# A linear-attention and mixer kernel with another order: token weights before the fourth pair's rows, four banks for the mixers, a later end for the zero products, other seeds

## Chip, cores and metric

The kernel runs on one core of a Trainium2 chip. A core has five engines with a queue of instructions each: PE (TensorE: matmuls, with a separate row PEld for its weight loads), ACT (ScalarE), DVE (VectorE), POOL (GpSimd) and SP (SyncE, which here issues DMA transposes only). PE writes to PSUM, which has eight banks. The metric is the device time of one execution in microseconds (us); shown are medians of several executions.

## The reference, cut to what matters

Four batches of eight heads, 768 steps, 64 numbers a head. The first part is a linear attention with a decay for each head, the second a mixer over steps and then over channels:

```python
for t in range(S):                       # S = 768, per batch and head
    state = gamma * state + outer(k[t], v[t])
    y[t] = scale * q[t] @ state
x = y as [batch, 768, 512]               # the eight heads side by side
h = relu(x^T @ w_tok1) @ w_tok2          # w_tok1 768x256, w_tok2 256x768
u = x + h^T
out = u + relu(u @ w_ch1) @ w_ch2        # w_ch1 512x1536, w_ch2 1536x512
```

## The kernel before, in words

Steps are cut into 6 blocks of 128, heads into 4 pairs. Everything is float16 on its way into PE and float32 in PSUM. The work is written as operations (class Op), each with its engine (or a choice of engines), planned cost, what it depends on and the buffers and PSUM banks it takes.

The front of a batch and pair (function `front`) is: scale k by the decay (L443 on ACT or L445 on DVE); transpose k and q (L479, L477) and copy them out as kT and qT (L486); the block states k^T v (L501) and their running sum U (L510, L513), copied to r (L524); the products within a block (L550), masked to am (L564); Y from both (L580, L584), scaled to X (L598 on ACT, or L602 on DVE) and cast to x (L615). Then the token work: T1 = x with w_tok1 (L629, relu L639 or L641), T2 = with w_tok2 (L687, added to X at L694), cast to u (L702), transposed (L721) and copied out as uT (L727). For the third and fourth pair of the first batch ("turned") T2 is made already transposed (L654, L657) and copied to uT at L664. Pair p's T1 depends on the pair before having done its T2 where that has an L687; the second and third pair's do, the fourth's does not.

The back of a batch (function `back`) is the channel mixer: `widen` makes relu(u w_ch1) in 24 tiles (L777 on PE, L791 on ACT), `narrow` multiplies by w_ch2 (L819) and adds X (L828); for batches 2 and 3 `narrow_seven` does that with seven block products in place of eight (L896, L905). In the first batch a widen tile's products are planned as two halves, pairs 0 and 1 and pairs 2 and 3 (SPLIT).

All rows and weights are loaded by POOL's DMA queue, in the order in which `request` is called (L384 and L394 rows, L364 weights): k, q, v of each pair of the first batch, at most eight requests in flight. T1_AT and T2_AT say before which pair's rows the two token weights are requested; 4 is after the last. Then come the channel weights and the other batches' rows. For batches 2 and 3, SP transposes k, q and u by DMA.

PSUM banks come from sets by name (BANKS): the first batch's front takes banks 0 to 6, later fronts 0 to 4, the mixers 5 to 7; `narrow_seven` takes any of the eight. L550 of the later fronts takes four banks at once.

The order of all this is not written down but found when the program is built. `arrange` plans greedily: the operation that can start first, by priority. `replay` runs the planned order through a model with DMA landings and gives a planned time. This is repeated 16 times with landing times fed back, and then once for each seed in SEEDS: `shake` gives a random share of the operations a delay or a bias against an engine (what one seed sets stays for the next). The order with the least planned time is emitted. Each engine then executes its instructions strictly in that order.

At the very end (L1015 to L1025) products of zeros (L1023) are put into PE's order before an operation that the plan starts before F_ON ns with a planned gap over 400 ns before it: as many as fill 0.7 of the gap at 165 ns each. Their results are not used.

Of the kernel before, what the change touches and what calls it, by code (L numbers as in the profile page):

```python
# [18 lines left out]
def kernel(  # L19
# [31 lines left out]

    BUFS = dict(kf=6, qf=6, k16=3, v16=8, kT=4, qT=4, U=2, q16=3, r16=3, am=8, X=3, x16=5, h1=3, u16=3,
                uT=3, h2=2, o=4, w1=2)
    BANKS = dict(first=range(0, 7), front=range(0, 5), back=range(5, 8), seven=range(0, 8), fill=range(7, 8))
    SEM = 80
    XB, XU = 2, 2
    QH, TN = (1,), 2
    SEEDS = [20000, 20001, 20017, 20030, 20091, 20125]
    SPLIT, T1_AT, T2_AT = 1, 4, 4
    XS, M4 = 1, 3  # L60
    EARLY, BOTH_FIRST, SEVEN = 0, 1, 2
    ops = []
# [26 lines left out]
    def replay(order):  # L89
# [4 lines left out]
        for o in order:  # L94
# [3 lines left out]
            for s in o.takes:  # L98
                if s.tag in BANKS:
                    got.append(bank_of[s.bank])  # L100
# [82 lines left out]
    def arrange():  # L183
# [10 lines left out]
        def freed(slot):  # L194
            if slot is None:
                return 0
            if any(u.end is None for u in slot.users):
                return None
            return max(u.end for u in slot.users) + SEM

        while todo:
            best = []
            for op in todo:
# [7 lines left out]
                for s in op.takes:  # L211
                    if s.tag in BANKS:
                        got = [(t, i) for i in BANKS[s.tag] if i not in [x[1] for x in banks]
                               for t in [freed(bank_of[i])] if t is not None]
# [42 lines left out]
            for s in op.takes:  # L257
                if s.tag in BANKS:
                    s.bank = banks.pop(0)[1]
# [733 lines left out]
    def shake(seed):  # L993

        rng = random.Random(seed)
        share = rng.choice((0.005, 0.02, 0.06))
        for o in ops:
            if rng.random() < share:
                o.delay = rng.choice((0, 0, 200, 500, 1000, 2000))
                o.skew = {w[0]: rng.choice((0, 0, 300, 800)) for w in o.ways}  # L1000

    best = None
    for turn in range(16 + len(SEEDS)):
        if turn >= 16:
            shake(SEEDS[turn - 16])
        order = arrange()
# [4 lines left out]
    for o, o.start, o.end, o.eng, o.emit, at in best[1]:  # L1011
        for s, s.bank in zip(o.takes, at):
            pass
        order.append(o)
    FILL, F_ON, F_NS = 0.7, 30000, 165  # L1015
    spare, pe_at = None, 300
    for o in order:
        if o.eng == "PE":
# [37 lines left out]
```

## Time and profile before

| | us |
|---|---|
| median of 8 executions | 202.84 |
| lowest, highest | 202.35, 206.94 |
| the profiled execution | 202.35 |
| its span in the trace | 200.6 |
| PE, DVE, ACT, POOL busy | 192.0, 131.2, 111.6, 81.9 |

The page's rows of 40 slices, each some 5 us, show where the engines are busy (a digit is the busy share in tenths; 9 is 90% or more) and which share of TensorE's clock was granted:

```profile
PE   7979799999999999999999999999999999999991
PEld 3546587566777676656765566656767886567881
DVE  7359963018999998575797509476389984056972
ACT  3159786677898555538850583448766003775000
POOL 7997776388986953443381021212220100000100
PEclk9999999999999999999999999999999999999999
```

A busy PE in these rows includes the products of zeros: 63 matmuls of line L1023, the last of them at 29.6 us. In the waits listed for PE there are four entries:

```profile
PE bank L580 <- ACT r L524: 1.2, 4, 0.7
PE bank L1023 <- DVE zero L309: 1.1, 1, 1.1
PE bank L479 <- DVE k L445: 1.1, 1, 1.1
PE bank L777 <- ACT uT L727: 0.8, 1, 0.8
```

The columns are who waited for whom, us in total, how often, and the longest.

### The profile page before, as it was taken

The page shows a single profiled execution, that of the slowest core. Times are in us where ns is not written, and L with a number is a line of the kernel's source. Part 1 is how long each engine was busy: PE and PEld are TensorE (multiplying, and loading weights), DVE is VectorE, ACT ScalarE, POOL GpSimd, SP SyncE. Part 2 cuts the span into 40 slices and gives each one's busy share as a digit, 9 for nine tenths or more (in the row PEclk, how much of TensorE's full clock was granted, in tenths as well). Part 3 has the DMA queues.
Part 4 walks back from the last instruction along what each step waited for, and adds up shares of the span by engine and source line. Part 5 has one row for each costly group of instructions (what it writes and reads, how often), then busy time and mean ns, then how long its engine had stood idle before and what let it go on. Part 6 is the DMA issues. An engine that isn't in the chain of part 4 may idle for free.

```text
span 200.6 us, 5027 instructions
## 1 busy us (share of the span) xinstructions
PE 192.0 (96%) x2015; PEld 132.1 (66%) x2015; DVE 131.2 (65%) x344; ACT 111.6 (56%) x245; POOL 81.9 (41%) x114
## 2 busy tenths in 40 slices
PE   7979799999999999999999999999999999999991
PEld 3546587566777676656765566656767886567881
DVE  7359963018999998575797509476389984056972
ACT  3159786677898555538850583448766003775000
POOL 7997776388986953443381021212220100000100
PEclk9999999999999999999999999999999999999999
DMA  6999999999999999999999996360220052000143
GB/s 43 144 156 158 205 207 207 191 155 154 147 146 149 180 126 158 167 189 130 184 150 137 149 160 135 92 171 16 41 43 0 3 209 105 0 3 0 52 158 109
DMA packets 101607, 24.71 MB, mean 123 GB/s; under 512 B 94288, under 2 KB 98640, under 8 KB 101584
## 3 DMA queue, kind: packets, MB, share of 16 engines
q0 software_dynamic: 78784, 13.37, 100.6%
q1 hardware_dynamic: 19200, 4.72, 19.4%
q10 hardware_dynamic: 3600, 6.29, 10.4%
q8 instruction: 16, 0.26, 0.6%
q14 instruction: 7, 0.06, 0.1%
HBM read 26.74 MB, written 6.29 MB: 165 GB/s over the span
## 4 chain that ended last, share of the span: by engine, by line
PE 87%; ACT 6%; DVE 4%; issue 0%; DVEq 0%; ACTq 0%
PE bank L777 32%; PE bank L819 16%; PE bank L896 13%; PE bank L1023 5%; PE bank L629 5%; PE bank L687 5%; PE bank L550 3%; PE bank L584 2%; PE bank L580 2%; PE bank L501 2%; PE bank L479 2%; DVE am L564 1%; ACT X L598 1%; ACT r L524 1%; ACT uT L664 1%; ACT kT L486 1%
## 5 line engine op out<-in xcount | busy, mean ns | idle before, releaser
L777 PE MATMUL bank<-uT,wc 128*128 128x384 f16 x384 | 68.9, 326 | 0.8 <-ACT uT L727 0.8
L791 ACT ACTIVATE h<-bank 128x384 f16<-128x384 f32 x96 | 46.8, 491 | 30.0 <-PE bank L777 29.4
L777 PEld LDWEIGHTS <-wc 128*128 128x128 f16 x384 | 35.5, 98 | 22.3 <-issue 1.0
L564 DVE TENSOR_TENSOR am<-bank,mask 128x384 f16<-128x384 f32 x64 | 33.1, 550 | 5.4 <-PE bank L550 5.4
L819 PE MATMUL bank<-wc,h 128*128 128x512 f16 x144 | 36.4, 379 | 0.0
L615 POOL CAST x<-X 128x384 f16<-128x384 f32 x25 | 12.7, 509 | 35.8 <-ACT X L598 31.9
L598 ACT ACTIVATE X<-bank,gy 128x192 f32<-128x192 f32 x58 | 20.7, 421 | 5.0 <-PE bank L584 4.6
L694 DVE TENSOR_TENSOR X<-X,bank 128x384 f32<-128x384 f32 x28 | 14.3, 550 | 12.8 <-PE bank L687 12.6
L702 POOL CAST u<-X 128x384 f16<-128x384 f32 x22 | 11.0, 512 | 23.1 <-DVE X L694 23.1
L819 PEld LDWEIGHTS <-h 128*128 128x128 f16 x144 | 12.7, 98 | 10.3
L513 DVE SCALAR_TENSOR_TENSOR U<-U,gp,bank 128x64 f32<-128x64 f32 x64 | 17.7, 276 | 1.1
L524 ACT ACTIVATE r<-U 64x320 f16<-64x320 f32 x27 | 12.6, 467 | 10.1 <-DVE k L445 5.2
L384 POOL DMA_DIRECT2D kf<-in_k_dram x16 | 16.6, 1039 | 2.9 <-DMA qf<-in_q_dram 1.4
L905 POOL TENSOR_TENSOR o<-X,o 128x256 f32<-128x256 f32 x2 | 1.5, 726 | 39.5 <-DVE o L905 39.5
L384 POOL DMA_DIRECT2D v<-in_v_dram x16 | 16.5, 1032 | 1.8 <-DMA wc<-in_moe_w_ch_dram 1.4
L1023 PE MATMUL bank<-zero 128*128 128x384 f16 x63 | 14.6, 384 | 1.1 <-DVE zero L309 1.1
L896 PEld LDWEIGHTS <-h 128*128 128x128 f16 x144 | 14.1, 98 | 2.1
L584 PEld LDWEIGHTS <-am 128*128 128x128 f16 x192 | 12.3, 98 | 4.1 <-issue 1.6
L584 PE MATMUL bank<-v,am 128*128 128x64 f16 x192 | 14.2, 193 | 0.0
L629 PE MATMUL bank<-x,wt 128*128 128x128 f16 x192 | 13.2, 219 | 0.0
L580 PE MATMUL bank<-r,qT 128*128 128x128 f16 x80 | 11.9, 220 | 1.2 <-ACT r L524 1.2
L629 PEld LDWEIGHTS <-wt 128*128 128x128 f16 x192 | 11.7, 98 | 2.0 <-DVE uT L727 0.3
(89 smaller groups left out, 275.4 us busy)
## 6 DMA issues: line engine op xcount, KB each, us to landing
out_dram<-o ACTq DMA_DIRECT2D x23, 256.0 KB, 2.9
kf<-in_k_dram POOLq DMA_DIRECT2D x16, 192.0 KB, 8.6
v<-in_v_dram POOLq DMA_DIRECT2D x16, 192.0 KB, 8.5
wc<-in_moe_w_ch_dram POOLq DMA_DIRECT2D x6, 512.0 KB, 14.5
qf<-in_q_dram POOLq DMA_DIRECT2D x12, 192.0 KB, 8.9
wt<-in_moe_w_tok_dram POOLq DMA_DIRECT2D x2, 384.0 KB, 9.6
qf<-in_q_dram POOLq DMA_DIRECT2D x8, 96.0 KB, 8.3
out_dram<-o ACTq DMA_DIRECT2D x2, 128.0 KB, 1.9
```

Source lines behind the costliest of these rows:

```text
L384: nc.gpsimd.dma_start(out=tile_of(s, [P, 2, NC, D], F16), in_=src[b, 2 * p:2 * p + 2].rearrange("h (c p) d -> p (h c) d", p=P))
L513: nc.vector.scalar_tensor_tensor(U[:, c], U[:, c - 1], gp[:, p:p + 1], o, ALU.mult, ALU.add)
L564: nc.vector.tensor_tensor(am[:, :m], src, k_, ALU.mult)
L580: nc.tensor.matmul(o, QT.tile[:, c * P:(c + 1) * P], R[:, c - 1], start=True, stop=False)
L584: nc.tensor.matmul(o[:, j * D:(j + 1) * D], M.tile[:, m], V.tile[:, j, c], start=(c == 0), stop=(c == 0 or j == 1))
L598: nc.scalar.mul(X.tile[:, half(hf), h * D:(h + 1) * D], yv[:, :, j * D:(j + 1) * D], gy[:, h:h + 1])
L629: nc.tensor.matmul(acc[:, jt * P:(jt + 1) * P], wt1[:, i, jt * P:(jt + 1) * P], X16.tile[:, i], start=(i == 0), stop=(i == NC - 1))
L777: nc.tensor.matmul(acc[:, :SH], w[:, ct, (ft % FW) * P:(ft % FW + 1) * P], UT.tile[:, ct, sh * SH:(sh + 1) * SH], start=(ct == 0), stop=(c ...
L791: nc.scalar.activation(H2.tile[:, ft], A.tile[:, :SH], AF.Relu)
L819: nc.tensor.matmul(A.tile, H2.tile[:, ft, i * P:(i + 1) * P], wc2[ft // FW][:, ft % FW], start=(opens and ft == 0), stop=(ft == NF - 1), s ...
L896: nc.tensor.matmul(bank.tile[:, cols], lhs(f, t), rhs(f), start=(f == 0 and not adds), stop=(f == HF - 1), skip_group_check=adds)
L1023: nc.tensor.matmul(spare[:, :384], zero[:, :P], zero, start=True, stop=True)
```

## The change

It sets five constants. No operation is added or removed apart from products of zeros, whose number follows from the plan.

```diff
-    BANKS = dict(first=range(0, 7), front=range(0, 5), back=range(5, 8), seven=range(0, 8), fill=range(7, 8))
+    BANKS = dict(first=range(0, 7), front=range(0, 5), back=range(4, 8), seven=range(0, 8), fill=range(7, 8))
...
-    SEEDS = [20000, 20001, 20017, 20030, 20091, 20125]
-    SPLIT, T1_AT, T2_AT = 1, 4, 4
+    SEEDS = [10003, 10006, 10008, 10011, 10016, 10019, 10024, 10029, 10031, 10038, 10039, 10043,
...
+    SPLIT, T1_AT, T2_AT = 1, 3, 4
...
-    FILL, F_ON, F_NS = 0.7, 30000, 165
+    FILL, F_ON, F_NS = 0.7, 36000, 165
```

The list of seeds goes from 6 to 48 entries, none in common. The mixers' set of banks becomes 4 to 7; bank 4 stays in the later fronts' set too, so both draw on it. The first token weights are requested before the fourth pair's rows of the first batch and after the third's; the second token weights stay where they were, after the fourth's. Products of zeros are put into gaps that the plan has before 36 us instead of 30 us.

## Prediction

> **What bounds the kernel now.** I read the page first (busy shares, slices), then the busy time by stretches of the span, then the chain of waits in order of time, then the timeline of the first 36 us, then the landings of single loads. The stretches, cut at places that the chain gives (columns: stretch, its length, then busy time and instruction count of PE, PEld, DVE, ACT, POOL, then clock, DMA share, GB/s):
>
> ```profile
> 0.00:9.65 9.65, 8.52 (x37) 4.45 (x38) 5.39 (x35) 2.30 (x4) 8.52 (x13) 1.00 1.42 91
> 9.65:25.00 15.35, 12.86 (x223) 8.66 (x221) 12.45 (x38) 11.51 (x24) 12.66 (x17) 1.00 2.20 172
> 25.00:30.00 5.00, 4.82 (x80) 4.15 (x78) 3.10 (x9) 4.11 (x12) 3.50 (x7) 1.00 1.24 207
> 30.00:35.57 5.57, 4.80 (x68) 4.03 (x66) 1.76 (x4) 3.89 (x8) 3.92 (x6) 1.00 1.24 207
> 35.57:196.60 161.03, 160.96 (x1619) 110.77 (x1618) 108.03 (x259) 89.83 (x198) 53.26 (x74) 1.00 1.25 115
> 196.60:200.60 4.00, 0.00 (x0) 0.00 (x0) 0.47 (x2) 0.00 (x0) 0.00 (x0) 1.00 0.37 131
> ```
>
> From 35.57 us on PE is busy 160.96 of 161.03 us. It waits for nobody there, and its instructions are the same before and after the change, so that stretch can only get longer. The last 4.00 us are the last addition and its store. What can shrink is the time before 35.57. Of the 25.92 us from 9.65 to 35.57 PE is busy 22.48 and idle 3.44; 29 of its matmuls there are products of zeros, which follow each other at about 0.165 us when nothing else comes between: 4.8 us. So 8.2 us of PE are unused by the program: that is the ceiling of any gain. (The 34 zero products before 9.65 precede the first transpose, whose rows the change doesn't touch.) What fills those 8.2 us is the chain of waits (start, length, what):
>
> ```profile
> 28.03 0.22 PE bank L580
> 28.76 0.67 PE bank L629 x12
> 29.43 0.49 PE bank L1023 x3
> 29.92 0.34 PE bank L721 x6
> 30.26 0.71 PE bank L687 x12
> 30.97 1.34 PE bank L629 x24
> 32.31 0.35 PE bank L654 x2
> 32.86 0.48 ACT uT L664
> ...
> 34.82 0.71 ACT uT L727
> 35.57 9.10 PE bank L777 x55
> ```
>
> After the last pair's Y (L580/L584, done at 28.76) PE still owes the token work of pair 1 (L629, L687), pair 0's transpose (L721) and pair 2's L629, before pair 3's L629 and L654; then ACT copies uT five times in a row. The backlog exists because token work began late:
>
> ```profile
> 25.32 0.83 PE L629 MATMUL bank<-x,wt 128*128 128x128 f16 x12
> 25.99 1.14 PE L1023 MATMUL bank<-zero 128*128 128x384 f16 x6
> 26.96 0.83 PE L687 MATMUL bank<-h,wt 128*128 128x128 f16 x12
> ```
>
> Pair 0's L629 starts at 25.32, though its x was cast by 20.30 (the DVE cast L615 at 19.76 took 0.54): what it lacked was the first token weights. Landings, from two looks at single requests (the fourth pair's q and v, issued at 11.71 and 12.72, and the first token weights, issued at 13.72):
>
> ```profile
> DMA to landing us min/median/max: 7.9/8.2/8.5
> DMA to landing us min/median/max: 9.0/9.0/9.0
> ```
>
> So v of pair 3 landed at 21.2 and the weights at 22.7. By the same query k landed at 18.3, q at 19.6 and the second token weights at 24.6.
>
> **Part 1, the request moved (T1_AT 4 to 3).** The first token weights pass k, q and v of pair 3. Landings in POOL's queue follow one another, and the weights occupied it for 22.7 - 21.2 = 1.5 us; so they land near 18.4, and k, q, v of pair 3 near 19.8, 21.1 and 22.7. Nothing behind them moves. On POOL the three row requests (1.1 us each) start 0.9 us later, the time of the weights' issue; the next other work on POOL is the cast at 18.27, so no one waits. No more than eight requests are in flight, and the ones to wait for had landed by 11.4: no wait. Who takes pair 3's rows: k was scaled at 20.46 (2.2 us after landing), q transposed at 21.75 (2.2 after), v used at 22.79 (1.6 after). All three margins exceed 1.5, v's by 0.1 only. If the planner, which sees later rows, also places pair 3 later, up to 1.5 us are lost: bounds 0 to 1.5, I take 0.8, because no trace shows the new order.
> A rule speaks against this part. The Trainium skill, DMA: Bandwidth & Descriptors, section "Anatomy of one DMA — SWDGE (gpsimd) path", gives a load of this kind about 2.0 us plus its bytes over 436 GB/s: for these 384 KB an estimate of 2.9 us. The trace has 1.5 between landings in a filled queue. With 2.9, k, q and v would come 0.7 to 1.3 us after the moments they are now used, and most of the gain would go. I take the trace's 1.5.
> The gain: pair 0's L629 (0.67) and its relu (0.40) go into holes between 20.3 and 25 (PE idles 0.67 before 24.75 alone). ACT and DVE are nearly full there (4.04 and 4.73 of 5), so the relu costs others up to 0.4; that is in the 0.8. L687 of pair 0 then needs the second token weights, 24.6, not the relu that ended at 26.81: up to 2.2 us earlier. L629 of pair 1 depends on it, so it and one or two groups more (0.67, 0.34 to 0.71) take the place of six zero products and the idle 0.4 before pair 3's Y. The backlog behind Y falls from 3.5 us (28.6 to 32.1) by about half. The limit is then pair 3 itself: x cast by 30.40 (DVE L615 at 29.85, 0.55), L629 0.67, relu 0.45, two L654/L657 groups 0.5 each, last copy 0.48, waits of about 0.1 between: mixers at full rate from some 33.1 instead of 35.57, -2.4 us. Less the 0.8: **-1.6**.
>
> **Part 2, four banks for the mixers (bank 4 shared with the fronts).** In the first batch a mixer's tile may begin with the products of pairs 0 and 1 and hold its bank until pairs 2 and 3 are there; one such half is 2 x 0.165 = 0.33 us. With three banks three halves fit, with four, four; before, pair 1's uT was the last (35.52), so none was done early but one matmul. With pair 1 early I count one or two halves that fill holes while pair 3 finishes: **-0.4** (bounds -1.3, 0). After 35.57 a fourth bank has no wait to remove. It can add some: each later front's L550 takes four banks at one moment, and of its five one may now be held by a mixer until its ACT eviction (0.49) is over. There are 12 such groups. Behind a waiting L550 stands all of PE, and then DVE's mask products and Y. Bounds 0 to 12 x 0.49 = 5.9; before, these 161 us hold 0.07 of idle, so orders with almost no wait exist, and I take **+0.3**.
>
> **Part 3, zero products planned until 36 us.** They come in front of a PE operation with a planned gap over 400 ns; each costs 0.165. From the one visible hole of that time (0.77 before 35.57) I take 3: 0.5 if the hole is not there on the chip, 0 if it is: **+0.3**. What could they buy? The Trainium skill, TensorE: Matmul & The Clock Gate, section "HAM oscillation — how this bites in real kernels", wants no PE pause over 3.4 us lest the clock drop to half. By that rule and by the trace the benefit is nothing: the longest pause after 9.65 us is 1.06, before 14.05, and after the 0.77 pause the mixers run at 9.10/55 = 0.165 each, as later. Zero products already delay real work: three of them stand in the chain at 29.43.
>
> **Part 4, the seeds.** Another list of random delays, so another order on every engine, before and after 35.57, with the same operations. Bounded above by the 8.2 us, below by waits inside the 161 us. More orders tried (64 against 22) may find a shorter planned front; the plan is not the chip. I take **+0.1**, and carry +-1.5 in the range.
>
> Sum: -1.6 - 0.4 + 0.3 + 0.3 + 0.1 = -1.3 us. The profiled execution took 202.35 (span 200.60 and 1.75 around it): 201.05. The median shown is 0.49 above it: **201.5**.
>
> **The rivals.**
> A, the sum above, 200.4 to 202.2 : chance 0.40.
> B, the move is hidden. L629 of pair 1 waits for L687 of pair 0, that for the second token weights, and these land at 24.6 as before; if the planner's order keeps L687 where it is, only 0.67 us of PE work shifts, and zero products take its place. For it: the six zeros at 25.99 come from a plan. Against: L687 was released by the relu, not by weights. Time 202.3 to 203.4; 0.24.
> C, slower: bank 4. PE stands before L550 while a mixer's eviction holds the fourth bank. Without the +0.3 the sum is -1.6: 1.6/0.49, three to four full waits of the twelve, eat the gain, and (1.6 + 2.0)/0.49, eight of them, lose 1% over before. It could also starve the fronts: batch 2's last uT landed at 125.1, 7 us before its mixer begins (132.4); more delay than that is PE idle. Against: PE has mixer work to put in between. Time 203.5 to 206; 0.15.
> D, slower: pair 3 pays its whole 1.5, the backlog gain is lost behind DVE, which is full until 27, and zeros cost 0.5: 202.35 + 1.5 + 0.5 - 0.4 + 0.49 = 204.4; 0.07.
> E, all fits: the 2.4 and 0.6 of early halves and no loss: 199.8; 0.14.
>
> **How the numbers follow.** Within 1% (about what a measurement of this kernel can tell from no change) means 200.8 to 204.9. Faster: E and a third of A, 0.28. Slower: half of C and a third of D, and some room for an order with waits of its own, 0.16. Same: 0.56. The range for 8 in 10 goes from 199.4 (below E's middle) to 204.6 (into C and past D).
>
> **What would show it.** Pair 0's L629 near 20.5 to 22 (part 1), L687 of pair 0 before 26; full-rate L777 from 33 to 34.5 rather than 35.57; some L777 pieces before the last L654; k of pair 3 scaled not later than 21. PE idle after the front under 0.5 us (C false), or waits of L550 or L777 on ACT's L791 (C true). Zero products in the chain after 30 us show part 3 costs. If the span falls and the front does not, or L629 stays at 25, my account is wrong.

## The result and the profile after

The changed kernel takes 201.95 us in the median of 16 executions; the kernel before, run beside it on the same chip, 204.11 in the median of 47. The ratio of the two is 0.9923, with a 95% interval of [0.9899, 0.9946]: about 1.6 us faster. Ratios, here and below, leave out executions more than 1.5% above the quickest of the same kernel; the medians do not. The profiled execution took 202.02 us, its span is 200.2. Behind the list of seeds, lines lie three further down in the changed kernel: L629 is now L632, L687 is L690, L777 is L780, and the products of zeros are L1026.

The busy time by stretches, cut at the same events as before (columns as there: stretch, length, busy time and instructions of PE, PEld, DVE, ACT, POOL, clock, DMA share, GB/s):

```profile
0.00:9.25 9.25, 8.13 (x37) 4.31 (x38) 5.39 (x35) 2.30 (x4) 8.12 (x13) 1.00 1.42 90
9.25:25.00 15.75, 14.37 (x248) 10.02 (x246) 11.87 (x36) 12.97 (x29) 12.84 (x17) 1.00 2.04 174
25.00:30.00 5.00, 5.00 (x83) 4.38 (x81) 4.96 (x14) 2.22 (x6) 3.18 (x6) 1.00 1.24 206
30.00:34.22 4.22, 4.22 (x50) 3.20 (x47) 1.60 (x3) 2.55 (x8) 3.03 (x5) 1.00 1.24 208
34.22:196.20 161.98, 160.94 (x1617) 111.04 (x1614) 103.57 (x250) 91.91 (x204) 56.11 (x77) 1.00 1.23 115
196.20:200.20 4.00, 0.00 (x0) 0.00 (x0) 0.53 (x2) 0.00 (x0) 0.00 (x0) 1.00 0.36 131
```

The mixers run without a break from 34.22 us instead of 35.57. And the long stretch behind is no longer full: PE is busy 160.94 of 161.98 us. The front in the timeline (start, length, instruction):

```profile
20.32 0.83 PE L632 MATMUL bank<-x,wt 128*128 128x128 f16 x12
21.00 1.30 PE L1026 MATMUL bank<-zero 128*128 128x384 f16 x7
...
25.17 0.82 PE L1026 MATMUL bank<-zero 128*128 128x384 f16 x4
25.83 0.83 PE L690 MATMUL bank<-h,wt 128*128 128x128 f16 x12
...
32.26 1.14 PE L780 MATMUL bank<-uT,wc 128*128 128x384 f16 x6
33.24 0.49 PE L657 MATMUL bank<-wt,h_all 128*128 128x384 f16 x2
...
34.22 7.96 PE L780 MATMUL bank<-uT,wc 128*128 128x384 f16 x48
```

Pair 0's token work starts at 20.32 us (25.32 before). Six matmuls of the mixers, three halves of a tile, come at 32.26, before the last L657; before the change one did. With this early work taken off, the mixers stand as if they had begun at 34.22 - 6 x 0.165 = 33.2 us, against 35.57 - 0.165 = 35.4: 2.2 us gained in the front, 0.4 of which is a first transpose that came 0.39 earlier (9.09 for 9.48) in this execution. The span is shorter by 0.4 only, because 1.04 us of idle time stand where before showed 0.07, and because of smaller gaps that the busy row hides: between the starts of PE's matmuls, waits over 0.13 us after 36 us sum to 1.9 us, where this profile of before has none.

The same sum works in all fourteen profiles of this case: PE's last matmul ends 160.9 to 161.4 us after the moment at which the mixers stand, plus these waits. So an execution is made of three parts: the first transpose (at 8.1 to 9.6 us), the front from there, and the waits behind it. The middle part is what tells the kernels apart. It takes 25.6 to 26.3 us in the five profiles with the front of before, and 24.1 to 24.5 in the eight with the changed one; the fourteenth is an experiment told below.

**The profile of before was a lucky one.** The span that the prediction was built on, 200.6 us, belongs to the quickest of before's executions. One more profile of the same kernel (span 203.2 us, first transpose at 8.70, mixers at 34.57):

> The kernel before, unchanged, profiled once more. If its usual execution (0.5 to 1 us above its first profile) differs from that profile by PE's waits on casts in the stretch from 45 to 75 us, they show here: 0.5 us or more of idle PE after 36 us, against 0.07 in the first profile. If it differs by the first stretch instead, the first transpose starts later than 9.5 us or the mixers later than 35.6.

Busy time from 60 to 80 us, in the first profile of before, in the second, and in the changed kernel:

```profile
60.00:80.00 20.00, 20.00 (x258) 13.72 (x257) 18.96 (x48) 12.84 (x27) 13.26 (x18) 1.00 2.17 155
```

```profile
60.00:80.00 20.00, 17.10 (x217) 11.54 (x216) 17.06 (x40) 10.66 (x25) 12.09 (x16) 1.00 2.25 155
```

```profile
60.00:80.00 20.00, 19.14 (x238) 12.89 (x235) 16.30 (x44) 11.52 (x25) 13.62 (x19) 1.00 2.13 151
```

The same program idles 0.0 or 2.9 us there. Who it waits for, in the second profile, for the window from 60 to 76 us (who, for whom, us in total, times, longest), first PE's waits, then ACT's and POOL's:

```profile
PE bank L501 <- ACT X L598: 2.0, 1, 2.0
PE bank L721 <- DVE am L564: 0.9, 1, 0.9
```

```profile
ACT q L452 <- DMA qf<-in_q_dram: 4.2, 1, 4.2
```

```profile
POOL kf L384 <- DMA qf<-in_q_dram: 4.0, 1, 4.0
```

These are read together. q of batch 2's third pair landed at 72.90 us here and at 67.14 in the first profile. ACT's next instruction is its cast, so ACT stands for 4.2 us; an X (L598) is queued behind it on ACT, and PE's L501 waits for that. POOL's next request may go out only when the eighth before it has landed, and stands too. So a row that is not needed for a long time stops an engine whose later instructions are needed now. SP's DMA transposes begin at 60 to 61 us. In the first profile the rows land 1.3 to 1.5 us after one another up to the q at 67.14, and the next three only at 72.6, 77.4 and 83.4; that the transposes make them late is likely, but no run here takes the transposes away.

### The profile page after: what moved, and what is told of

Same layout as the page of the kernel before. It is cut to its first block, busy times and chain, and to the rows that moved or that the text cites. A ratio compares the mean times of both kernels' runs of the same rounds, so it can differ in the third digit from the quotient of the medians.

```text
span 200.2 us, 5036 instructions
## 1 busy us (share of the span) xinstructions
PE 192.7 (96%) x2020; PEld 133.0 (66%) x2020; DVE 127.9 (64%) x338; ACT 111.9 (56%) x248; POOL 83.3 (42%) x115
## 4 chain that ended last, share of the span: by engine, by line
PE 78%; POOL 9%; ACT 5%; issue 3%; DVE 2%; DVEq 0%; POOLq 0%
PE bank L780 30%; PE bank L822 13%; PE bank L899 13%; PE bank L1026 5%; PE bank L632 4%; PE bank L690 4%; POOL qf L387 2%; POOL v L387 2%; PE bank L553 2%; POOL kf L387 2%; PE bank L587 2%; PE bank L583 1%; PE bank L504 1%; ACT X L601 1%; ACT r L527 1%
## 5 line engine op out<-in xcount | busy, mean ns | idle before, releaser
L780 PE MATMUL bank<-uT,wc 128*128 128x384 f16 x384 | 67.4, 326 | 0.0
L794 ACT ACTIVATE h<-bank 128x384 f16<-128x384 f32 x96 | 45.7, 490 | 23.8 <-PE bank L780 22.9
L780 PEld LDWEIGHTS <-wc 128*128 128x128 f16 x384 | 36.0, 98 | 22.1
L567 DVE TENSOR_TENSOR am<-bank,mask 128x384 f16<-128x384 f32 x64 | 33.1, 551 | 7.3 <-PE bank L553 7.2
L601 ACT ACTIVATE X<-bank,gy 128x192 f32<-128x192 f32 x54 | 19.3, 420 | 8.4 <-PE bank L587 8.1
L705 POOL CAST u<-X 128x384 f16<-128x384 f32 x23 | 11.8, 530 | 29.3 <-DVE X L697 29.3
L527 ACT ACTIVATE r<-U 64x320 f16<-64x320 f32 x29 | 13.6, 468 | 7.1 <-DVE U L516 6.7
L446 ACT ACTIVATE k<-kf,gk 128x384 f16<-128x384 f16 x22 | 12.7, 609 | 6.6 <-DMA kf<-in_k_dram 5.2
L1026 PE MATMUL bank<-zero 128*128 128x384 f16 x68 | 15.2, 372 | 1.1 <-DVE zero L312 1.1
L632 PE MATMUL bank<-x,wt 128*128 128x128 f16 x192 | 13.6, 219 | 0.0
L632 PEld LDWEIGHTS <-wt 128*128 128x128 f16 x192 | 12.0, 98 | 2.3 <-DVE am L567 0.2
```

The costliest lines, as they stand in the source:

```text
L527: nc.scalar.mul(RS.tile[r, :, r], US.tile[r], g128[2 * p + j])
L567: nc.vector.tensor_tensor(am[:, :m], src, k_, ALU.mult)
L601: nc.scalar.mul(X.tile[:, half(hf), h * D:(h + 1) * D], yv[:, :, j * D:(j + 1) * D], gy[:, h:h + 1])
L632: nc.tensor.matmul(acc[:, jt * P:(jt + 1) * P], wt1[:, i, jt * P:(jt + 1) * P], X16.tile[:, i], start=(i == 0), stop=(i == NC - 1))
L780: nc.tensor.matmul(acc[:, :SH], w[:, ct, (ft % FW) * P:(ft % FW + 1) * P], UT.tile[:, ct, sh * SH:(sh + 1) * SH], start=(ct == 0), stop=(c ...
L794: nc.scalar.activation(H2.tile[:, ft], A.tile[:, :SH], AF.Relu)
```

## The experiments

Two theories stood against mine (the early request clears the backlog of token work): that the other seeds had found a better order, and that the fourth bank did it. Four constants differ between the kernels: the place of the first token weights, the mixers' banks, the seeds and the end of the zero products.

**The request alone.**

```diff
-    SPLIT, T1_AT, T2_AT = 1, 4, 4
+    SPLIT, T1_AT, T2_AT = 1, 3, 4
```

(in the kernel before; seeds whose delays leave the planner with no startable operation are skipped)

> The kernel before with the first token weights requested before the fourth pair's rows, and nothing else of the change (delays under which the planner finds no order are passed over). Theory 1, the token backlog: the gain comes from this request, so most of it is here: 1.0 to 2.2 us faster than before, pair 0's first L629 near 20.5 us, mixers at full rate by 34.5 us. Theory 2, the other seeds: within 0.4 us of before. Theory 3, the fourth bank for early halves of the mixers' tiles: within 0.5 us of before or slower.

Ratio to before 0.9963 [0.9929, 0.9997], some 0.75 us. Its trace:

```profile
21.19 0.83 PE L629 MATMUL bank<-x,wt 128*128 128x128 f16 x12
...
26.66 0.83 PE L687 MATMUL bank<-h,wt 128*128 128x128 f16 x12
...
33.09 1.14 PE L777 MATMUL bank<-uT,wc 128*128 128x384 f16 x6
...
35.05 1.21 PE L777 MATMUL bank<-uT,wc 128*128 128x384 f16 x6
```

The front has the changed kernel's form: the token work from 21.19, three halves early with three banks, the mixers standing at 35.05 - 0.99 = 34.1 us, 1.3 before the kernel before (1.4 when both are counted from their first transpose). PE's order is that of the changed kernel up to its first difference, the fourth half tile, behind the last L657. The 0.8 us by which this trace is later than the changed kernel's arise earlier: 0.45 before the first transpose, and another 0.42 by pair 0's token work, where the orders are still the same. So the mechanism is shown in the front. In the time, 0.75 us (by the interval 0.1 to 1.4) of the change's 1.6 are shown for the request by itself, less than the 1.0 to 2.2 that I expected; waits over 0.13 us sum to 1.1 us behind this front.

**The bank alone, and the seeds undone.**

```diff
-    BANKS = dict(first=range(0, 7), front=range(0, 5), back=range(5, 8), seven=range(0, 8), fill=range(7, 8))
+    BANKS = dict(first=range(0, 7), front=range(0, 5), back=range(4, 8), seven=range(0, 8), fill=range(7, 8))
```

> The kernel before with bank 4 open to the mixers, and nothing else. Theory 1: no gain in front, since pair 1's uT comes as late as before, and waits of PE after the front: 0 to 2.5 us slower than before. Theory 3: 0.4 to 1.3 us faster than before.

Ratio 1.0025 [0.9990, 1.0061], from 9 of its 20 executions (the median of all is 205.86, of before 203.96): no gain. The front has no early half beyond the one matmul of before, as theory 1 has it; behind it are 2.8 us of waits. The mixers come at 34.06 us all the same, but only because the first transpose came at 8.25: from there the front takes 25.6 us, as in before.

The changed kernel with the six seeds of before in place of its 48:

> The changed kernel with the six seeds of before. Theory 1: the front keeps its gain (full-rate mixers by 34.5 us), but the order after it pays for the shared bank with waits of PE: 0.5 to 2.5 us slower than the changed kernel. Theory 2: the gain is gone in front too, mixers at full rate only at 35.5 us. Theory 3: within 0.4 us of the changed kernel.

Ratio to before 0.9899 [0.9843, 0.9956], so as quick as the changed kernel, as far as four executions tell. The front was kept, as expected, but the expected price was not paid. PE's orders with 6 and with 48 seeds are the same up to some 97 us of the traces. The long list of seeds changes only what comes after, where PE is full in every trace, and bought nothing that can be measured, although the planner's own time falls from 201.6 to 199.6 us with it.

**The request put back.**

```diff
-    SPLIT, T1_AT, T2_AT = 1, 3, 4
+    SPLIT, T1_AT, T2_AT = 1, 4, 4
```

> The changed kernel with the first token weights requested after the fourth pair's rows again. Theory 1: most of the gain goes, within 0.6 us of before, first L629 at 25 us. Theories 2 and 3: still 1.0 to 1.6 us faster than before.

Ratio to before 0.9972 [0.9915, 1.0029]: with bank and seeds kept and the request undone, no gain over before can be told. Only 4 of its 20 executions are in this ratio, and the interval alone does not exclude the 1.0 us of the rivals; but the median of all twenty is 206.72 us, above the 203.96 of before. The trace (of an execution of 206.02 us) decides for the front: L632 comes at 24.24, no half is early, and from the first transpose, at 8.06, the front takes 26.3 us. Together with the bank alone and the six seeds, this makes both rivals fall as causes of the gain in front.

Behind the front, PE stands for 3.65 us in this trace, and not for the shared bank:

```profile
72.03 0.36 DVE L457 COPY q<-qf 128x768 f16<-128x768 f16 x1 [3.76 <-DMA qf<-in_q_dram]
74.00 0.84 PE L632 MATMUL bank<-x,wt 128*128 128x128 f16 x12 [3.65 <-DVE am L567]
```

DVE's cast waits for a late q, the masks (L567) stand behind it on DVE, and PE behind these: what the second profile of before shows, on a third engine.

**The request moved and the order held.** All engines keep the changed kernel's order; only POOL asks for the weights behind the fourth pair's rows:

```diff
+    t1 = wops["t1"]
+    order.remove(t1)
+    order.insert(order.index(loads[0, NP - 1][2][1]) + 1, t1)
     FILL, F_ON, F_NS = 0.7, 36000, 165
```

> The order of the changed kernel on every engine, but the first token weights are requested after the fourth pair's rows. Theory 1, that order lives on the early weights: pair 0's L632 waits until 22.8 us or later, everything behind it on PE too, mixers at full rate 0.5 to 1.5 us later, the kernel 0.4 to 1.5 us slower than the changed one. Rival, the order alone makes the gain: within 0.3 us of the changed kernel.

Ratio to before 1.0049 [1.0021, 1.0077]. Against the changed kernel that is 1.0049/0.9923, 1.3% or 2.6 us slower; I had said at most 1.5. The timeline (the inserted lines move the products of zeros to L1029), and the stretch from 24 to 28 us:

```profile
23.25 0.87 PE L632 MATMUL bank<-x,wt 128*128 128x128 f16 x12 [2.21 <-DMA wt<-in_moe_w_tok_dram]
23.93 2.43 PE L1029 MATMUL bank<-zero 128*128 128x384 f16 x7
26.15 0.85 PE L482 MATMUL bank<-ident,k 128*128 128x128 f16 x6
```

```profile
24.00:28.00 4.00, 4.00 (x39) 2.53 (x37) 0.36 (x1) 2.51 (x6) 0.51 (x1) 0.58 1.23 206
```

PE stands 2.21 us before L632, all else behind it. Then the clock is at half for 3.4 us from 23.9 (0.58 over the window), and the seven products of zeros, which took 1.30 us in the changed kernel, take 2.43 in front of pair 3's transpose. The mixers come at 38.48 us, 4.3 later than in the changed kernel; in this profile no wait follows behind, so that less of it is seen in the time. The order lives on the early weights.

The reverse: before's order with the early request.

```diff
+    t1 = wops["t1"]
+    order.remove(t1)
+    order.insert(order.index(loads[0, NP - 1][0][1]), t1)
     FILL, F_ON, F_NS = 0.7, 30000, 165
```

> The order of the kernel before on every engine, but the first token weights are requested before the fourth pair's rows. Theory 1: nothing uses the early weights, L629 stays at 25.3 us, and pair 3's rows come 1.5 to 3 us later against margins of 1.6 to 2.2: 0 to 1.2 us slower than before. Rival, early weights help by themselves: 0.5 us faster or more.

The front is before's to 0.1 us: L629 at 25.38, mixers at 35.63. Nothing used the weights early. Pair 3's rows came some 2 us later (k at 20.5) and just used up the margins that the prediction read off the trace: ACT stood 0.30 us for k and scaled it at 20.57 instead of 20.46. Yet the ratio is 0.9942 [0.9917, 0.9967], 1.2 us faster where I expected no gain or a loss. That is the number of the rival, and by the ratios alone this kernel can't be told from the changed one. The quickest executions tell them apart: 202.39 us here and 202.35 in before, but 201.78 with the request alone and 201.22 in the changed kernel. The changed front moves this floor; the early request in the old order only keeps the time close to it (the slowest of its 14 executions took 203.33). Its profile has no wait after 36 us, like the first profile of before, so it seems to escape the late rows more often. Why one request at 11 us should change that is open; nothing was tried to settle it.

**The products of zeros.**

```diff
-    FILL, F_ON, F_NS = 0.7, 36000, 165
+    FILL, F_ON, F_NS = 0.7, 9000, 165
```

> The changed kernel with products of zeros before the first transpose only (34 of 68). Theory 1, these products delay real work and keep nothing warm: 0.2 to 0.9 us faster than the changed kernel, pair 0's L690 at 25.2 instead of 25.8 us, granted clock as before. Rival, they keep the clock up through the front: executions with a granted clock near 0.991 (3.4 us at half rate) appear, and the time is 0.5 to 2 us longer.

The median is 201.51 us, the ratio to before 0.9872 [0.9835, 0.9908], at least as quick as the changed kernel (their intervals overlap). Three stretches of its trace:

```profile
8.00:13.40 5.40, 3.50 (x60) 2.55 (x59) 2.10 (x7) 2.01 (x3) 5.40 (x6) 1.00 2.38 152
13.40:20.30 6.90, 5.85 (x97) 5.19 (x98) 5.75 (x18) 5.92 (x12) 5.37 (x8) 0.51 2.17 169
...
30.00:36.00 6.00, 6.00 (x73) 4.63 (x72) 2.41 (x5) 4.11 (x12) 4.21 (x6) 1.00 1.24 207
```

The clock does drop, as the rival said, to half for 6.8 us. It costs next to nothing, as the rival did not say: in that stretch ACT and DVE are busy 5.9 and 5.8 of 6.9 us, and PE is not what is waited for; from the first transpose the front takes 24.4 us, 0.3 more than in the changed kernel's profile. The clock is back before the mixers begin. My own expectation was wrong on the clock and on L690, which stayed at 25.92 us.

**The waits behind the front.** First, the request in front of two u casts on POOL put behind them:

```diff
+    casts = [o for o in order if o.eng == "POOL" and o.prio in ((0, 1, 2, 30), (0, 1, 2, 33))]
+    late = loads[3, 0][2][1]
+    order.remove(late)
+    order.insert(max(order.index(o) for o in casts) + 1, late)
```

> The changed kernel with one row request on POOL (v of batch 3, pair 0) put behind the two u casts that it stood in front of near 69 us; nothing else. Theory 1, PE's 1.2 us of waits at 70 us come from that request, which waits for an earlier landing while the casts queue behind it: these waits fall below 0.3 us and the kernel is 0.6 to 1.2 us faster than the changed one. Rival, the shared bank 4 causes them: the waits stay and the time is within 0.3 us of the changed kernel.

A miss: 0.9913 [0.9874, 0.9952], no different from the changed kernel. The wait for the u casts is gone, and another is there (PE's waits from 36 to 100 us, in the slowest of nine executions):

```profile
PE bank L632 <- POOL x L618: 2.4, 2, 1.2
PE bank L504 <- ACT h L642: 0.5, 1, 0.5
```

The request now stands in front of the x casts. So three requests of batch 3 were put behind all casts of batch 1:

```diff
+    last = [o for o in order if o.eng == "POOL" and not o.dma and o.prio[:2] == (0, 1)][-1]
+    late = [o for o in order if o in queue and o.prio[:2] == (0, 3) and 67500 < o.start < last.start]
+    for o in late:
+        order.remove(o)
+    at = order.index(last) + 1
+    order[at:at] = late
```

> The changed kernel with three row requests of batch 3 (v of pair 0, k and q of pair 1) put behind the casts of batch 1 that follow them on POOL, up to 77 us. Theory 1, PE's waits between 60 and 75 us come from casts queued behind requests that wait for a landing: waits of PE on POOL below 0.3 us, the kernel 0.7 to 1.5 us faster than the changed one. Rival, the fourth bank is what PE waits for there: waits and time within 0.3 us of the changed kernel.

Ratio 0.9888 [0.9840, 0.9935], median 201.58 us. PE waits on POOL no more. But in this profile, of the slowest of six executions, ACT stood 3.12 us for a late k, the relu behind it, and PE 1.02 us behind that:

```profile
82.36 1.12 ACT L446 ACTIVATE k<-kf,gk 128x384 f16<-128x384 f16 x2 [3.12 <-DMA kf<-in_k_dram]
...
83.80 0.83 PE L690 MATMUL bank<-h,wt 128*128 128x128 f16 x12 [1.02 <-ACT h L642]
```

The cause is the one seen in before, with another engine in the middle. The fourth bank, the rival, is in none of the waits that were followed up. The changed kernel has two short waits of PE before L504 for a PSUM bank, 0.3 us at 53 us and 0.2 at 59; both banks (0 and 1) belong to the fronts alone, and the second came free late because ACT had waited 0.41 us for a late k. Last, the same with fewer products of zeros: none planned after 24 us, and none but the first 34.

> As requests_behind, and no products of zeros planned after 24 us (60 instead of 68; the eight that go stand before L690 of pairs 0 and 1). Theory 1: they delay those by 0.3 to 0.6 us, so this is 0.2 to 0.6 us faster than requests_behind, granted clock unchanged. Rival, they keep the clock up: executions with a clock near 0.991 appear.

> As requests_behind, with products of zeros before the first transpose only. Theory 1 as fewer_zeros showed: the clock falls to half for 3.4 to 6.8 us within the front, where PE is not what is waited for, and the time is within 0.4 us of behind_24. Rival, the half clock costs its full 1.7 to 3.4 us: slower than behind_24 by over 1 us.

0.9876 [0.9831, 0.9920] and 0.9860 [0.9812, 0.9909], medians 201.43 and 201.15 us. The three can't be told apart by their intervals, so the 0.2 to 0.6 us for the fewer products are not shown; but the last is not the 1 us slower that the rival asked for. It has the lowest median of all kernels here (measured apart from the changed one, beside 204.28 for before), its clock at half for 3.4 us in the front of its profile, and 198.8 us as its span.

## Why the prediction was right, point by point

The time, 201.5 us as 1.3 below the profiled 202.35 plus 0.49, is a ratio of 201.5/202.84 = 0.993; 0.992 was measured. That it is so near is in part luck: of the five terms only the first was found on the chip, and the other four, -0.4, +0.3, +0.3 and +0.1, happen to sum to no more than +0.3.

- **Part 1, -1.6 us.** The mechanism holds in the front: T1 at 20.32, pair 0's L690 at 25.83 (I had said before 26), six L780 before the last L657, and the gain gone when the request is undone. Full rate at 34.22 (33 to 34.5) shows little: with the bank alone and with the request put back it came at 34.06 and 34.40, after an earlier first transpose. L690 was 1.1 us earlier, not up to 2.2. Two other signs failed: k of pair 3 was scaled at 21.48, not by 21, and PE idles 1.04 us behind the front, not under 0.5. The size in the front is 1.4 in the trace of the request alone and 1.8 in the changed kernel, both from the first transpose on. The loads were mis-sized. In the changed kernel the weights, k, q and v of pair 3, issued at 10.71, 11.52, 12.52 and 13.53, took from issue to landing:

```profile
DMA to landing us min/median/max: 9.1/9.1/9.1
DMA to landing us min/median/max: 9.7/9.7/9.7
DMA to landing us min/median/max: 9.5/9.5/9.5
DMA to landing us min/median/max: 9.7/9.7/9.7
```

  That is 19.8, 21.2, 22.0 and 23.2 us, for my 18.4, 19.8, 21.1 and 22.7. The weights landed 3.1 us after the v in front of them, not 1.5; the 2.9 estimated from the Trainium skill (DMA: Bandwidth & Descriptors, "Anatomy of one DMA — SWDGE (gpsimd) path") was nearer here. With the request alone they came 1.4 after v, and k 3.1 after them. So the difference of two landings is not what one load occupies. The four together took 6.5 us (6.3 with the request alone, 5.8 before). And the loss that I tied to a 2.9 us load didn't come: pair 3's Y did end 1.0 us later than before (29.79 for 28.76), but with the backlog gone, that was paid from the gain.
- **Part 2, -0.4 us.** Wrong in its cause. Halves are done early, but three, and three banks hold three; the request alone shows them too. In the front nothing is left that the fourth bank is seen to give.
- **Part 3, +0.3 us.** It was nothing. No gap in the plan between 30 and 36 us exceeds 0.38 us, so raising the limit adds no product of zeros: the request alone, with the limit at 30 us, has the same 68, and the last of them is at 27.7 us in the changed kernel. With the request put back the hole is there again, and five stand in it at 33.4 us.
- **Part 4 and the bank's +0.3.** The seeds change nothing before 97 us, and nothing that can be measured after. Waits after the front did appear, 1.9 us, but as late rows in front of casts, and before has them too (3.5 us in its second profile).
- **The first step, that the stretch after 35.57 us "can only get longer".** As a least length this holds in every profile. Wrong was to take it for what before needs: it rested on one execution without a wait, while another of the same program idles 2.9 us there. The sum came out all the same because before and after both pay such waits as a rule, which the prediction did not know.

Not settled: where the rest of the 1.6 us comes from beyond the 0.75 of the request alone, and what the bank's other order after 35 us gives (the changed kernel and the request alone have overlapping intervals, 0.9899 to 0.9946 and 0.9929 to 0.9997); and why before's order with the early request is quicker.

## What to carry to other kernels

A request moved ahead in a shared queue is worth what the planned order can use: the same early weights gave nothing to the front of an order made for late ones, and the order made for them lost 2.6 us without them. A stretch that looks full in one profile may not be so in the next; before counting on it, profile the kernel twice and ask which in-order engine has an instruction at its head that waits for a transfer. Two profiles are best compared from an event that both share: here the first transpose alone moved by 1.5 us between executions, as much as the gain. Filling a front with dummy products is worth testing by leaving them out: here the clock that they hold up did not matter where PE was not what the others waited for.

## What the runs showed of the hardware

The granted clock fell to half without a long pause of PE. In the kernel with 34 products of zeros the longest pause before 13.4 us was 1.0 us, and PE was busy 3.50 of 5.40 us; it then ran at half clock from 13.5 to 20.3. In the changed kernel, with PE busy 5.01 of the same 5.40 us, it did not fall. With a pause of 2.21 us (the order held, the request late) it fell for 3.4 us. In the three traces where it falls before the mixers, such a stretch is one or two times 3.41 us long. But with the request put back, PE paused for 3.65 us, and the clock stayed full (1.00, the third number from the right):

```profile
68.90:75.70 6.80, 3.15 (x38) 1.94 (x37) 3.52 (x11) 0.82 (x3) 1.84 (x3) 1.00 1.46 193
```

PE is busy 46% of this stretch, less than the 65% after which the clock fell elsewhere. So neither the longest pause nor the busy share says in these traces when it falls; what does is open. The pause of 3.4 us that I had taken from the Trainium skill (TensorE: Matmul & The Clock Gate, "HAM oscillation — how this bites in real kernels") as the limit was not reached where the clock fell, and was passed where it did not.

The end of the 34 first products also moves with the clock. They are issued from 1.1 us on; their weight loads follow one another at 0.32 us until full speed is granted and at 0.16 after, and that change comes at 6.9 us in the first profile of before and at 4.0 with the request put back. The first transpose behind them came at 9.48 and 8.06, and between 8.06 and 9.60 in all profiles. Its k had been scaled by 6.9 us, so in these kernels the first transpose waits for products of zeros; no run tries fewer than 34.
